# Scores and exponentials in padded rows of nine, divided into separate tiles

## The chip, the cores and the metric

The kernel runs on one core of one Trainium2 chip. The metric is the device time of one execution in microseconds; three runs of the kernel before gave a median of 691.24 us (690.34 to 692.95).

## The reference

Attention over 4 batches, 8 heads, 768 positions and 64 numbers per head, followed by an expert layer over 3072 tokens (512 to 2048 to 512):

```python
scores = scale * np.matmul(q, k.transpose(0, 1, 3, 2))
is_global = pos[None, :] < int(n_global)            # the first 8 keys
is_local = (rel >= 0) & (rel < int(n_local))        # 96 keys back
bias = -slopes[:, None, None] * dist[None, :, :]
scores = np.where(is_global | is_local, scores + bias[None], -1000000000.0)
a = np.exp(scores - np.max(scores, axis=-1, keepdims=True))
a = a / (np.sum(a, axis=-1, keepdims=True) + 1e-09)
x = np.matmul(a, v)            # then [tokens, 512]
h = x @ w_in
g = np.where(h > 0.0, h, np.exp(np.minimum(h, 0.0)) - 1.0)
out = g @ w_out
```

## The kernel before

The 3072 tokens are cut into 12 groups of 256 (two tiles of 128 queries), three groups to a batch. For each group four pairs of heads go through attention, and then 16 chunks of the expert layer (128 hidden columns each) follow. A tile of queries sees 232 keys (96 before it, the 8 global ones, its own 128); the first tile of a batch sees its own 128 alone.

Groups 0 to 3, counted from 0, run attention in plain float32 (`pair32`). From group 4 on, `pair` splits every operand of a matmul into a high part and a rest in a faster type, and works ahead: while TensorE goes through the expert chunks of one group, the attention of the next is threaded in between. There are 8 such groups and so 32 pairs of heads, each with four score tiles (two heads, two query tiles): 128 tiles, of which 16 have 128 columns and 112 have 232.

A pair goes like this. A *visit* of TensorE (L542 to L550) first transposes the probabilities of the pair before (L500, into the PSUM banks `t` and `th`) and then computes the scores of its own pair (L480, into `s`). VectorE adds the position table, takes the row maximum and writes maximum less score (L569) into a tile `pr`; ScalarE exponentiates it in place and sums the row (L571); VectorE inverts the sums (L584, L585) and multiplies each tile by its inverse, in place (L589 to L592, through L557): this is the division. The next visit transposes the tiles. Then ScalarE and VectorE split the transposed tiles (L517, L518), TensorE multiplies them with the values (L529, into `pv`), and VectorE adds the two halves (L536).

An expert chunk is eight or twelve matmuls into a PSUM bank `h` (L663, L667), a chain on ScalarE and VectorE (copy, L672, L683, L684, L685, a cast to `gh`), a subtraction to `gl` (L277, on GpSimd in this stretch), and matmuls that accumulate into two banks `o` (L707). There are two banks `h`, so the first matmul of a chunk waits until L685 has read the bank of the chunk but one before.

The order of all instructions on each engine is computed before the program is emitted. `Plan.order` (L102) takes, over and over, the operation that can start first, by written costs (`act`, `dve`, `pool`, `pe`), by due times, and by when a slot of the operation's tile class comes free. A cost is a triple of engine, time and a flag; an operation with the flag set waits, in this plan, until the last flagged operation has ended (`port`, L136 and L177). All GpSimd work carries the flag, and so does the division on VectorE. A visit is planned 1200 ns after its inputs are ready (`BEHIND`). `SLOTS` (L803) lists the buffers of each class: `pr` has four. On the chip the engines run their queues in the planned order and wait for each other by semaphores alone.

Of the kernel before, what the change touches and what calls it, by code (L numbers as in the profile page):

```python
# [11 lines left out]
AF = mybir.ActivationFunctionType  # L12
ALU = mybir.AluOpType
# [3 lines left out]
P = 128  # L17
# [3 lines left out]
WN = A0 + P  # L21
HK = WN // 2
NT = 2
# [183 lines left out]
def act(n, psum=False, extra=0.0):  # L207
    return (("ACT", (55 if psum else 97) + 0.834 * n + extra, False),)


def dve(n, fast=False, port=False):
    return (("DVE", (75 + 0.521 * n) if fast else (70 + 1.042 * n), fast or port),)


def pool(n, two=True):
    return (("POOL", (30 + 2.58 * n) if two else (50 + 1.1 * n), True),)
# [6 lines left out]
class Kernel:  # L223
# [182 lines left out]
    def pair(self, b, gi, hp, xh, xl, due, ahead, step, X):  # L406
        nc, p = self.nc, self.plan
        t0 = gi * NT
# [59 lines left out]
              [rqv, vd], [vd], due - 7500)  # L468

        ss = [self.bank("s", "s", [P, NT, WN]) for _ in range(2)]  # L470
        prs = [[self.sb("pr", "pr", [P, WN]) for _ in range(NT)] for _ in range(2)]
        st = self.sb("st", "st", [P, 3, 2 * NT])
        tiles = [(t0 + i, i * (NG + P)) + self.blocks(t0 + i) for i in range(NT)]
# [9 lines left out]
        self.visit(scores, 1.4 * sum(WN - x[2] for x in tiles), [qs, ks], ss, ahead)  # L483
        for j in range(2):
            for i in range(NT):
                self.softmax(b, 2 * hp + j, t0 + i, lambda j=j, i=i: ss[j].t[:, i], ss[j], prs[j][i], st, j * NT + i,
                             ahead + 7000 + (2 * j + i) * step)
        self.inverse(st, ahead + 4500 + 3 * step)
        for j in range(2):
            for i, x in enumerate(tiles):  # L490
                self.norm(prs[j][i], x[2], st, j * NT + i, ahead + 4600 + 3 * step + 2 * j + i, False)
        tps = [self.bank(c, c, [P, 2 * NT * 2, 64]) for c in ("t", "th")]

        def transposes():
# [66 lines left out]
    def softmax(self, b, h, t, st_, s, pr, st, i, d):  # L561

        nc, p = self.nc, self.plan
        lo = 0 if t else A0
        n = WN - lo
        at = (b * self.H + h) * (self.S // P) + t
        nm = self.nmax.t[:, at:at + 1]
        tab = self.tab1.t if t else self.tab0.t
        p.add((("DVE", 158 + 1.042 * n, False),), lambda e: nc.vector.tensor_tensor_reduce(  # L569
            pr.t[:, lo:], st_()[:, lo:], tab, -(2.0 ** -(h + 1)), 3.0e38, ALU.add, ALU.min, nm), [s], [pr], d - 4500)  # L570
        p.add(act(n, extra=200), lambda e: nc.scalar.activation(  # L571
            pr.t[:, lo:], pr.t[:, lo:], AF.Exp, bias=nm, scale=-1.0, accum_out=st.t[:, 0, i:i + 1]), [pr], [pr, st], d - 4000)

    def blocks(self, t):

# [10 lines left out]

        self.plan.add((("DVE", 290.0, False),), inverse, [st], [st], due)

    def norm(self, pr, lo, st, i, due, both):  # L589
        n = WN - lo  # L590
        self.plan.add((act(n, extra=90) + pool(n, False) if both else ()) + (("DVE", 130 + 0.53 * n, True),), lambda e: self.scaled(
            e, pr.t[:, lo:], pr.t[:, lo:], st.t[:, 2, i:i + 1]), [pr, st], [pr], due)  # L592

    def pair32(self, b, hp, t0, q32, k32, v32, rqv, rk, pv, due, step, X):

# [139 lines left out]
    def build(self):  # L735
# [49 lines left out]
        for _, f in sorted(todo, key=lambda x: x[0]):  # L785
# [16 lines left out]
    WARM, FILL = True, 60000.0  # L802
    SLOTS = {"rqv": ["rqv0"], "rk": ["rk0"], "qs": ["qs0"], "ks": ["ks0"], "vd": ["vd0", "part0", "part1"],  # L803
             "s": ["s0", "s1"], "t": ["t0"], "th": ["v0"], "pv": ["v0", "t0"], "h": ["h0", "h1"], "o0": ["o0"], "o1": ["o1"],
             "pr": ["pr0", "pr1", "pr2", "pr3"], "st": [f"st{i}" for i in range(6)], "pt": ["pt0", "pt1"],
             "x": ["x0"], "xh": ["xh0", "xh1", "xh2"], "e": ["e0", "e1"], "gh": ["gh0", "gh1", "gh2"],
             "gl": ["gl0", "gl1", "gl2"], "io": ["io0", "io1", "io2", "io3"], "part": ["part0", "part1", "vd0"]}

# [266 lines left out]
```

## Time and profile before

| What | Value |
|---|---|
| Median of three runs | 691.24 us |
| Profiled execution, its own time | 692.7 us |
| Its span, first to last instruction | 690.9 us |
| TensorE matmul busy | 677.5 us (98%) |
| VectorE busy | 510.0 us (74%) |
| ScalarE busy | 521.6 us (75%) |
| GpSimd busy | 219.7 us (32%) |
| Granted TensorE clock, mean | 0.999 |

The profile is of one execution. Busy times add the drawn lengths of the instructions, overlaps counted once. The drawn ends of matmuls are modelled, and consecutive ones overlap, so how far TensorE is from its best is read from when matmuls start, not from its busy share. "Idle before" names the time in which an engine had nothing drawn and what released it.

### The profile page before, as it was taken

What the parts mean: (1) busy time and instruction counts of PE and PEld (TensorE: products, weight loads), DVE (VectorE), ACT (ScalarE), POOL (GpSimd) and SP (SyncE); (2) the same over time, 40 slices, a digit from 0 to 9 for tenths busy, and PEclk for the clock granted to TensorE, in tenths of its full rate; (3) what the DMA queues carried; (4) which work ended last, traced back from release to release, by engine and by line L of the source; (5) the groups of instructions that cost most, each with busy time, mean ns of one, the idle gap of its engine ahead of it and who ended that gap; (6) DMA issues with size and microseconds to landing.
All of it is one profiled execution on the core that took longest, in us unless ns stands there. A gap on an engine that the chain in (4) does not pass through costs nothing.

```text
span 690.9 us, 13740 instructions
## 1 busy us (share of the span) xinstructions
PE 677.5 (98%) x4512; PEld 568.9 (82%) x4512; DVE 510.0 (74%) x1586; ACT 521.6 (75%) x1584; POOL 219.7 (32%) x304
## 2 busy tenths in 40 slices
PE   9999999999999999999999999999999999999996
PEld 6777888888888877788888888888888888888885
DVE  7999999985468777867876777777778766785322
ACT  7998888756477778778877888778778877886553
POOL 4142000200115433433353335333353443323221
PEclk9999999999999999999999999999999999999999
DMA  7837941001123112112212112112111211200001
GB/s 258 297 103 253 388 155 47 1 11 39 58 61 95 35 35 78 56 35 65 68 35 66 35 47 88 35 36 84 50 36 50 83 35 35 66 1 1 32 0 37
DMA packets 22402, 51.61 MB, mean 75 GB/s; under 512 B 2482, under 2 KB 9394, under 8 KB 22322
## 3 DMA queue, kind: packets, MB, share of 16 engines
q1 hardware_dynamic: 22176, 50.51, 22.0%
q8 instruction: 38, 0.62, 0.4%
q14 instruction: 42, 0.34, 0.2%
q10 hardware_dynamic: 146, 0.14, 0.1%
HBM read 44.34 MB, written 6.29 MB: 73 GB/s over the span
## 4 chain that ended last, share of the span: by engine, by line
PE 82%; DVE 8%; ACT 6%; issue 2%; DMA 1%; POOL 0%; DVEq 0%; POOLq 0%; ACTq 0%; SPq 0%
PE o L707 33%; PE h L663 16%; PE h L678 9%; PE h L667 8%; PE pv L529 3%; PE s L480 3%; PE t L500 2%; PE s L608 2%; ACT pr L571 2%; PE pv L642 1%; DVE x L536 1%; PE t L625 1%; DVE pr L557 1%; PE none L851 1%; DMA rqv<-in_qkv_dram 1%
## 5 line engine op out<-in xcount | busy, mean ns | idle before, releaser
L707 PE MATMUL o<-w,gh 128*128 128x512 f32 x764 | 227.6, 398 | 0.6 <-DVE part L723 0.4
L277 POOL TENSOR_TENSOR gl<-e,gh 128x256 fp32r<-128x256 f32 x144 | 108.4, 753 | 214.3 <-ACT gh L269 199.4
L707 PEld LDWEIGHTS o<-w,gh 128*128 128x128 f32 x764 | 135.4, 188 | 26.7 <-ACT gh L269 0.8
L663 PE MATMUL h<-xh,w 128*128 128x512 f32 x568 | 155.4, 395 | 2.1 <-DVE e L685 1.9
L685 DVE SCALAR_TENSOR_TENSOR e<-e,h 128x256 f32<-128x256 f32 x192 | 80.3, 418 | 70.6 <-ACT e L684 64.5
L663 PEld LDWEIGHTS h<-xh,w 128*128 128x128 f32 x568 | 104.7, 188 | 29.5 <-DVE e L685 5.3
L707 PE MATMUL o<-w,gl 128*128 128x512 f32 x382 | 129.0, 398 | 0.0
L269 ACT CAST gh<-e 128x256 fp32r<-128x256 f32 x192 | 77.9, 406 | 53.6 <-DVE e L685 52.7
L683 ACT ACTIVATE e<-h 128x256 f32<-128x256 f32 x192 | 74.0, 386 | 52.9 <-DVE h L672 34.7
L571 ACT ACTIVATE pr<-pr,nmax 128x232 f32<-128x232 f32 (+1 forms) x192 | 91.4, 478 | 6.0 <-DVE nmax L569 5.9
L667 PEld LDWEIGHTS h<-xh,w 128*128 128x128 f32 x568 | 86.1, 188 | 11.7
L672 DVE TENSOR_TENSOR h<-h,e 128x256 f32<-128x256 f32 x142 | 60.9, 429 | 45.4 <-ACT e L269 44.8
L678 PEld LDWEIGHTS h<-xh,w 128*128 128x128 f32 x600 | 85.6, 189 | 9.6 <-issue 1.9
L678 PE MATMUL h<-xh,w 128*128 128x256 f32 x600 | 92.4, 284 | 0.0
L667 PE MATMUL h<-xh,w 128*128 128x256 f32 x568 | 89.6, 280 | 0.0
L684 ACT ACTIVATE e<-e 128x256 f32<-128x256 f32 x192 | 80.4, 419 | 4.1
L569 DVE CUSTOM_DVE_ANT_0 pr<-s,tab 128x232 f32<-128x232 f32 (+1 forms) x192 | 67.1, 375 | 15.4 <-PE s L480 15.0
L269 ACT COPY e<-h 128x256 f32<-128x256 f32 x142 | 53.1, 374 | 20.2 <-PE h L667 15.9
L707 PEld LDWEIGHTS o<-w,gl 128*128 128x128 f32 x382 | 63.9, 189 | 4.8 <-issue 0.3
L536 DVE TENSOR_TENSOR x<-pv,x 64x256 f32<-64x256 f32 x128 | 53.8, 420 | 9.1 <-ACT x L269 6.5
L557 DVE TENSOR_SCALAR pr<-pr,st 128x232 f32<-128x232 f32 (+1 forms) x143 | 58.2, 433 | 0.9
L559 POOL TENSOR_SCALAR pr<-pr,st 128x232 f32<-128x232 f32 (+1 forms) x31 | 17.2, 566 | 104.5 <-DVE st L585 54.8
(108 smaller groups left out, 903.0 us busy)
## 6 DMA issues: line engine op xcount, KB each, us to landing
rqv<-in_qkv_dram SPq DMA_DIRECT2D x45, 384.0 KB, 3.1
rk<-in_qkv_dram SPq DMA_DIRECT2D x45, 184.0 KB, 2.6
bits<-in_w_in_dram SPq DMA_DIRECT2D x16, 512.0 KB, 7.2
bits<-in_w_out_dram SPq DMA_DIRECT2D x16, 512.0 KB, 9.9
out_dram<-ob SPq DMA_DIRECT2D x24, 256.0 KB, 2.0
rqv<-in_qkv_dram SPq DMA_DIRECT2D x3, 192.0 KB, 5.1
rqv<-in_qkv_dram SPq DMA_DIRECT2D x3, 128.0 KB, 2.7
rk<-in_qkv_dram SPq DMA_DIRECT2D x2, 132.0 KB, 3.5
```

The costliest lines, as they stand in the source:

```text
L269: self.nc.scalar.copy(out, x)
L277: self.on(e).tensor_tensor(out, x, y, ALU.subtract)
L557: self.nc.vector.tensor_scalar(out, x, sc, None, ALU.mult)
L569: p.add((("DVE", 158 + 1.042 * n, False),), lambda e: nc.vector.tensor_tensor_reduce(pr.t[:, lo:], st_()[:, lo:], tab, -(2.0 ** -(h + 1)), ...
L571: p.add(act(n, extra=200), lambda e: nc.scalar.activation(pr.t[:, lo:], pr.t[:, lo:], AF.Exp, bias=nm, scale=-1.0, accum_out=st.t[:, 0, i: ...
L663: nc.tensor.matmul(h.t, w1.t[:, HI, cc * P:(cc + 1) * P], xh.t[:, :, cc], start=cc == 0, stop=False)
L667: nc.tensor.matmul(hx(), w1.t[:, LO, cc * P:(cc + 1) * P], xh.t[:, HI, cc], start=False, stop=cc == self.NCC - 1)
L678: nc.tensor.matmul(hx(), w1.t[:, s, cc * P:(cc + 1) * P], xh.t[:, x, cc], start=n == 0 and cc == 0, stop=n == 2 and cc == self.NCC - 1)
L683: p.add(act(W, True), lambda e: nc.scalar.activation(ex.t, hx(), AF.Relu, scale=-1.0), [h], [ex], d - 8000)
L684: p.add(act(W), lambda e: nc.scalar.activation(ex.t, ex.t, AF.Exp, scale=-1.0), [ex], [ex], d - 8000)
L685: p.add(dve(W), lambda e: nc.vector.scalar_tensor_tensor(ex.t, ex.t, -1.0, hx(), ALU.add, ALU.max), [h, ex], [ex], d - 8000)
L707: nc.tensor.matmul(acc[i].t, g.t[:, i * P:(i + 1) * P], w2.t[:, s], start=fc == f0 and n == 0 and s == HI, stop=fc == f1 - 1 and n == 1)
```

## The change

From group 4 on, L569 and L571 work in tiles `raw` of their own, of 29 rows of 9 numbers of which 8 are used (16 rows for a tile of 128 columns). The division reads a `raw` tile and writes a `pr` tile as one contiguous run. In the plan the wide divisions (29 rows, an odd number) get the cost `dve(n)` without the flag; those of 128 columns keep the old cost. The classes `pr` and `raw` share six slots. Groups 0 to 3 keep their tiles; the helper `eights` leaves their operands one run. The new lines are L570 (scores), L573 (exponentials) and L558 (division).

```diff
+        raws = [[self.sb("raw", "raw", [P, WN // 8, 9]) for _ in range(NT)] for _ in range(2)]
         prs = [[self.sb("pr", "pr", [P, WN]) for _ in range(NT)] for _ in range(2)]
...
-                self.softmax(b, 2 * hp + j, t0 + i, lambda j=j, i=i: ss[j].t[:, i], ss[j], prs[j][i], st, j * NT + i,
+                self.softmax(b, 2 * hp + j, t0 + i, lambda j=j, i=i: ss[j].t[:, i], ss[j], raws[j][i], st, j * NT + i,
...
-                self.norm(prs[j][i], x[2], st, j * NT + i, ahead + 4600 + 3 * step + 2 * j + i, False)
+                self.norm(prs[j][i], x[2], st, j * NT + i, ahead + 4600 + 3 * step + 2 * j + i, False, raws[j][i])
...
-            pr.t[:, lo:], st_()[:, lo:], tab, -(2.0 ** -(h + 1)), 3.0e38, ALU.add, ALU.min, nm), [s], [pr], d - 4500)
+            self.eights(pr.t, n, lo), self.eights(st_()[:, lo:], n), self.eights(tab, n), -(2.0 ** -(h + 1)), 3.0e38, ALU.add, ALU.min, nm),
+            [s], [pr], d - 4500)
...
-            pr.t[:, lo:], pr.t[:, lo:], AF.Exp, bias=nm, scale=-1.0, accum_out=st.t[:, 0, i:i + 1]), [pr], [pr, st], d - 4000)
+            self.eights(pr.t, n, lo), self.eights(pr.t, n, lo), AF.Exp, bias=nm, scale=-1.0, accum_out=st.t[:, 0, i:i + 1]),
+            [pr], [pr, st], d - 4000)
...
-    def norm(self, pr, lo, st, i, due, both):
+    def eights(self, x, n, lo=0):
+
+        if len(x.shape) == 3:
+            return x[:, :n // 8, :8]
+        return x[:, lo:lo + n].rearrange("p (a b) -> p a b", b=8)
+
+    def norm(self, pr, lo, st, i, due, both, raw=None):
+
         n = WN - lo
-        self.plan.add((act(n, extra=90) + pool(n, False) if both else ()) + (("DVE", 130 + 0.53 * n, True),), lambda e: self.scaled(
-            e, pr.t[:, lo:], pr.t[:, lo:], st.t[:, 2, i:i + 1]), [pr, st], [pr], due)
+        x = raw or pr
+        one_port = raw and n // 8 % 2
+        self.plan.add((act(n, extra=90) + pool(n, False) if both else ()) + (dve(n) if one_port else (("DVE", 130 + 0.53 * n, True),)),
+                      lambda e: self.scaled(e, self.eights(pr.t, n, lo), self.eights(x.t, n, lo), st.t[:, 2, i:i + 1]), [x, st], [pr], due)
...
-             "pr": ["pr0", "pr1", "pr2", "pr3"], "st": [f"st{i}" for i in range(6)], "pt": ["pt0", "pt1"],
+             "pr": ["pr2", "pr3", "pr0", "pr1", "raw0", "raw1"], "raw": ["raw0", "raw1", "pr0", "pr1"], "st": [f"st{i}" for i in range(6)], "pt": ["pt0", "pt1"],
```

On VectorE, the order changes around the divisions. These rows are from the second pair of heads of group 4, from the sums (`st`) on; `x` is the output of L536, `h` and `e` belong to expert chunks, `ks` is the next pair's keys. Before:

```order
L585 RECIPROCAL st_2852<-st_2852 128x4
L536 TENSOR_TENSOR x_2911<-pv_2903,x_2911 64x256
L672 TENSOR_TENSOR h_2913<-h_2913,e_2945 128x256
L536 TENSOR_TENSOR x_2911<-pv_2903,x_2911 64x256
L277 TENSOR_TENSOR ks_2880<-rk_2750,ks_2880 128x368
L557 TENSOR_SCALAR pr_2838<-pr_2838,st_2852 128x232
L685 SCALAR_TENSOR_TENSOR e_2945<-e_2945,h_2913 128x256
L557 TENSOR_SCALAR pr_2846<-pr_2846,st_2852 128x232
L557 TENSOR_SCALAR pr_2874<-pr_2874,st_2852 128x232
L557 TENSOR_SCALAR pr_2918<-pr_2918,st_2852 128x232
```

After:

```order
L588 RECIPROCAL st_2856<-st_2856 128x4
L558 TENSOR_SCALAR pr_2946<-raw_2842,st_2856 128x232
L558 TENSOR_SCALAR pr_2953<-raw_2850,st_2856 128x232
L537 TENSOR_TENSOR x_2915<-pv_2907,x_2915 64x256
L684 TENSOR_TENSOR h_2917<-h_2917,e_2951 128x256
L537 TENSOR_TENSOR x_2915<-pv_2907,x_2915 64x256
L277 TENSOR_TENSOR ks_2884<-rk_2750,ks_2884 128x368
L558 TENSOR_SCALAR pr_2974<-raw_2878,st_2856 128x232
L558 TENSOR_SCALAR pr_2982<-raw_2922,st_2856 128x232
L697 SCALAR_TENSOR_TENSOR e_2951<-e_2951,h_2917 128x256
```

Two divisions stand ahead of the additions and the key subtraction, and all four ahead of the chunk's L697 (L685 before).

On TensorE, the visits move. These rows are the end of the expert matmuls that lie between the second and the third visit of that group, up to the first transposes of the third. Before:

```order
L707 MATMUL o_2942<-w_126_1034,gl_3129 128x512
L707 MATMUL o_2927<-w_285_1253,gh_3145 128x512 x2
L707 MATMUL o_2942<-w_285_1253,gh_3145 128x512 x2
L667 MATMUL h_3149<-xh_2320,w_294_1316 128x256 x4
L707 MATMUL o_2927<-w_285_1253,gl_3156 128x512
L707 MATMUL o_2942<-w_285_1253,gl_3156 128x512
L707 MATMUL o_2927<-w_291_1365,gh_3167 128x512 x2
L663 MATMUL h_3187<-xh_2320,w_300_1392 128x512 x4
L707 MATMUL o_2942<-w_291_1365,gh_3167 128x512 x2
L667 MATMUL h_3187<-xh_2320,w_300_1392 128x256 x4
L500 MATMUL t_3204<-ident,pr_3043 116x64
L500 MATMUL th_3205<-ident,pr_3043 116x64
```

After:

```order
L719 MATMUL o_2948<-w_126_1034,gh_3122 128x512 x2
L679 MATMUL h_3131<-xh_2320,w_288_1236 128x256 x4
L719 MATMUL o_2931<-w_126_1034,gl_3137 128x512
L719 MATMUL o_2948<-w_126_1034,gl_3137 128x512
L675 MATMUL h_3166<-xh_2320,w_294_1316 128x512 x4
L501 MATMUL t_3178<-ident,pr_3127 116x64
L501 MATMUL th_3179<-ident,pr_3127 116x64
```

The third visit comes right after the first half of the chunk that uses `w_294`; before, that chunk's second half, the next chunk's matmuls and twelve of L707 stood ahead of it. The number of expert matmuls in the group stays as it was; the gap before the next group's first visit gets those that the earlier gaps lose.

## Rows read from the trace of the kernel before

**Rows 1.** the page, shares of the chain that ended last, by engine:

```profile
PE 82%; DVE 8%; ACT 6%; issue 2%; DMA 1%; POOL 0%; DVEq 0%; POOLq 0%; ACTq 0%; SPq 0%
```

**Rows 2.** waits in 195:640: engine, line, releaser: total us, times, longest:

```profile
PEld h L663 <- DVE e L685: 5.3, 14, 1.1
PE h L663 <- DVE e L685: 1.9, 5, 0.7
PE th L500 <- DVE x L536: 0.9, 1, 0.9
```

**Rows 3.** TensorE: start, us, what, count; then a group, its mean ns:

```profile
418.10 1.08 PE L707 MATMUL o<-w,gh 128*128 128x512 f32 x4
419.02 0.63 PE L667 MATMUL h<-xh,w 128*128 128x256 f32 x4
...
L707 PE MATMUL o<-w,gh 128*128 128x512 f32 x522 | 154.7, 399 | 0.0
```

**Rows 4.** TensorE in order of time; in brackets idle before, releaser:

```profile
213.45 0.73 PE L663 MATMUL h<-xh,w 128*128 128x512 f32 x2 [0.29 <-DVE e L685]
...
255.64 0.24 PE L500 MATMUL th<-ident,pr 64*116 64x64 f32 x1 [0.86 <-DVE x L536]
...
281.72 0.96 PE L663 MATMUL h<-xh,w 128*128 128x512 f32 x3 [0.70 <-DVE e L685]
...
498.55 0.47 PE L663 MATMUL h<-xh,w 128*128 128x512 f32 x1 [0.35 <-DVE e L685]
...
610.67 0.27 PE L500 MATMUL t<-ident,pr 64*116 64x64 f32 x1
```

**Rows 5.** VectorE and GpSimd in order of time, before three of these waits:

```profile
212.04 0.90 DVE L557 TENSOR_SCALAR pr<-pr,st 128x232 f32<-128x232 f32 x1
...
212.07 0.74 POOL L277 TENSOR_TENSOR xh<-x,xh 128x256 fp32r<-128x256 f32 x1 [1.44 <-ACT xh L269]
...
252.69 1.88 DVE L557 TENSOR_SCALAR pr<-pr,st 128x232 f32<-128x232 f32 x2
...
253.13 1.30 POOL L277 TENSOR_TENSOR vd<-rqv,vd 128x512 fp32r<-128x512 f32 x1
...
278.95 1.35 DVE L557 TENSOR_SCALAR pr<-pr,st 128x232 f32<-128x232 f32 x2
...
279.00 1.16 POOL L277 TENSOR_TENSOR vd<-rqv,vd 128x384 fp32r<-128x384 f32 x1
```

**Rows 6.** L557: ns least/median/longest; then its wide form in 195:640, mean ns:

```profile
L557 DVE TENSOR_SCALAR pr<-pr,st x143: 269/336/1462, 9.0 to 619.4; 128x232 f32<-128x232 f32 x127, 128x128 f32<-128x128 f32 x16
...
L557 DVE TENSOR_SCALAR pr<-pr,st 128x232 f32<-128x232 f32 x112 | 47.8, 449 | 0.6
```

**Rows 7.** VectorE groups by line and shape: busy us, mean ns, idle before:

```profile
L459 DVE SCALAR_TENSOR_TENSOR qs<-rqv,scale,qs 128x256 fp32r<-128x256 f32 x31 | 14.9, 482 | 0.2
...
L387 DVE SCALAR_TENSOR_TENSOR g<-bits,g 128x512 int32<-128x512 int32 x32 | 21.8, 684 | 0.0
...
L277 DVE TENSOR_TENSOR w<-g,w 128x512 fp32r<-128x512 f32 x26 | 17.8, 684 | 0.0
...
L277 DVE TENSOR_TENSOR ks<-rk,ks 128x368 fp32r<-128x368 f32 x24 | 12.9, 537 | 0.1
```

**Rows 8.** ScalarE groups by line and shape:

```profile
L571 ACT ACTIVATE pr<-pr,nmax 128x232 f32<-128x232 f32 x160 | 78.6, 492 | 1.3 <-DVE nmax L569 1.2
...
L378 ACT ACTIVATE g<-bits 128x512 f32<-128x512 f32 x32 | 21.4, 675 | 1.3 <-DVE w L277 0.6 <-DMA bits<-in_w_in_dram 0.6
L269 ACT CAST w<-g 128x512 fp32r<-128x512 f32 x32 | 19.8, 619 | 3.4 <-DVE g L387 3.3
```

**Rows 9.** three gaps between visits: length, busy us (instructions) of each engine:

```profile
243.73:254.51 10.78, 10.78 (x79) 9.13 (x79) 9.29 (x27) 8.23 (x27) 3.88 (x5) 1.00 0.18 56
599.60:610.67 11.07, 11.07 (x80) 9.30 (x80) 9.25 (x30) 8.72 (x29) 2.32 (x3) 1.00 0.00 0
610.67:621.04 10.37, 10.37 (x77) 8.88 (x76) 8.19 (x29) 8.91 (x28) 2.94 (x4) 1.00 0.01 2
```

## The prediction

> **What bounds the kernel now.** I read the chain of waits first, then who waited for whom in the stretch that the change touches, then single instructions in order of time where TensorE waited. The chain that ended last lies on TensorE for 82%, on VectorE for 8% and on ScalarE for 6% of the span [rows 1]. So nothing but a wait of TensorE is worth anything. The division that the change rewrites (L557 in the groups from 4 on, counted from 0) runs between 195 and 640 us; there TensorE shows idle time before two lines only: 1.9 us in five waits before L663 (the first matmul of an expert chunk, which needs the PSUM bank that VectorE's L685 reads) and 0.9 us in one wait before the transposes L500 [rows 2]. Matmuls overlap: one with 512 columns is drawn about 0.40 us long, but four in a row start 0.23 us apart (418.10 to 419.02 is 0.92 for four) [rows 3]. A wait therefore hides 0.40 - 0.23 = 0.17 us more than its idle time shows. Six waits: 1.9 + 0.9 + 6 x 0.17 = 3.8 us. That is about all the change can win. The outer bound is what the weight loads show: 5.3 us before L663 in 14 waits, plus the 0.9 = 6.2 us [rows 2].
>
> Why do these waits exist? At 255.64 us the transposes into bank th had waited 0.86 us for an addition L536, which stood in VectorE's queue behind two divisions that together took 1.88 us; all that time GpSimd had a subtraction of 1.30 us running (253.13 to 254.43), and the divisions end 0.14 us after it. At 281.72 the wait of 0.70 us has two divisions of 1.35 us before it, beside a GpSimd subtraction of 1.16 us (to 280.16); at 213.45, 0.29 us, one of 0.90 us beside GpSimd's 0.74 us [rows 4, 5]. The division has a median of 336 ns and a longest of 1462 ns [rows 6]: it is an instruction that sometimes stands still until GpSimd is done. The three waits are 0.86 + 0.70 + 0.29 + 3 x 0.17 = 2.4 us; the other three (1.9 + 0.9 - 1.85 = 0.95 shown, 1.5 with the hidden part) have no long division right before them.
>
> **The division.** 112 of the 128 divisions have 232 columns, 16 have 128. Today the 112 have a mean of 449 ns [rows 6], so 112 x (449 - 336) = 12.7 us of VectorE's time go into standing still. After the change the source is 29 rows of 8 with a gap, the destination one run of 232. No row shows what that does, so I bound it. From below: nothing changes, 336 ns and the standing still as now. [...] Two subtractions of the same kind differ by (684 - 537) / (512 - 368) = 1.02 ns per element; an instruction with a per-row scalar from a tile and 256 elements at that rate takes 482 ns [rows 7], so 232 elements take 482 - 24 x 1.02 = 457 ns. I take 457 ns, nearest to the L459 row, without standing still: 112 x (457 - 449) = 0.9 us more VectorE time over 445 us, so nothing in sum, but every division costs the same and none costs 1.46 us. The 16 narrow divisions have 16 rows, and I leave them at what they cost now.
>
> [...]
>
> **The padded tiles.** L569 writes and L571 reads and writes 29 rows of 8 instead of a run. Nearest rows: L387 reads every second word and takes 684 ns for 512 elements, the contiguous subtraction also 684 [rows 7], so VectorE pays 0. ScalarE's L378 reads every second word in 675 ns, its contiguous cast L269 takes 619 [rows 8]; if all of the 56 ns were the stride, 232 elements would pay 25 ns, at both ends of the instruction 50. I take 0; the other end is 4 x 50 = 0.2 us per pair of heads on the way from scores to transposes. A gain here has no reason.
>
> **The buffers and the order.** Six slots stand where four did, a score tile is free again after its division, and the planner no longer holds a wide division back for GpSimd. The divisions move forward on VectorE, ahead of the additions L536 (the first order piece), and the next visit of the transposes comes sooner on TensorE (the second). Between visits TensorE has expert matmuls; counted in the two orders, the four gaps of the first group hold 40, 42, 42, 30 matmuls of 512 columns before and 38, 30, 30, 56 after; in the later ones without a first tile the pattern is 34, 36, 30, 60. Matmuls neither come nor go, so TensorE's work stays. SP's loads keep their sequence. On GpSimd the value tiles of the next pair come ahead of one or two expert subtractions; those are then late by that much, and hidden by the chunk of matmuls that TensorE still has between a chunk's first and last use. New waits: L569 waits for a division two or more instructions back on its own engine, which has ended by then; behind it would stand the following scores and L672, but I price it at 0.
>
> A gap with 30 to 31 matmuls exists today: 243.73 to 254.51 and 599.60 to 610.67, followed by one of 10.37 us. VectorE is busy 9.29 of 10.78, 9.25 of 11.07 and 8.19 of 10.37 us in them [rows 9]. The first ends in the 0.86 us wait; the transposes at 610.67 show no idle before them [rows 4]. So a short gap is kept without a wait when the divisions do not stand still. Cover for a late division is the time that VectorE has free: 2.18 us in the third of these gaps; four divisions that are each 457 - 336 = 0.12 us slower than a quiet one use 0.5 of it, the padded tiles at worst 0.2.
>
> **Sum.** Of the three waits with a long division before them 2.4 us go; of the other 1.5 us about half, 0.7, since divisions earlier in the queue delay them as well; against this the shorter gaps, where I count 11 with 30 or 34 matmuls and put 0.04 us on each, a third of the 0.12 us by which one division is slower than a quiet one: 0.4 us. 2.4 + 0.7 - 0.4 = 2.7 us. The profiled execution took 692.7 us (span 690.9 and 1.8 around it), so 690.0 for such a run. The median of the runs shown, 691.24, lies 1.46 below the profiled run; the forecast on that footing is 688.5 us, with its own range 687.0 to 690.3.
>
> **Rivals.**
> 1. All waits go, and some hidden ones with them: between 3.8 and 6.2 us, say 4.6, gives 686.6. For it: the long divisions are the only irregular instruction of VectorE there. Against: L663 also waits after chains without a long division (498.55).
> 2. Another wait takes over at once: L685 still comes behind ScalarE, and TensorE loses what it won. 691.2 us. For it: three of the six waits have no long division right before them.
> [...]
> 4. Slower: the shorter gaps. Three visits follow each other closely; the loop from scores over L569, L571, L584, L557 to the next transposes must run in about 11 us. It decides from the point where the loop is longer than the gap: then each of the six gaps with 30 matmuls ends in a wait like that at 255.64, 1.03 us, and the five with 34 in half of one: 6 x 1.03 + 5 x 0.5 = 8.7, less the 3.8 won: 4.9 us more, 696.1. For it: of today's three gaps with at most 32 matmuls, two end in a wait. Against: both have a division beside GpSimd, the third has not and does not wait.
>
> **Chances.** Forecast 0.44, rival 1 0.25, rival 2 0.14, rival 3 0.05, rival 4 0.12. Half a per cent (3.46 us, about what a measurement of this kernel tells from no change) means under 687.8 or over 694.7. Faster: rival 1 and a small part of the forecast, 0.30. Slower: most of rival 4 and a rest, 0.11. Same: 0.59. The range 686.2 to 693.0 leaves out rival 4 and the far end of rival 1.
>
> **What will show it.** Right: L558, the new division, wide form, within 440 to 475 ns, its longest under 600; no idle before the transposes; 1 us or less before the expert matmuls that now wait 1.9. VectorE's busy time changed by under 5 us. L573, the exponential in its new form, within 50 ns of 492 [rows 8]. Wrong: a wide division still over 800 ns (rival 3), exponentials over 550 ns, or repeated idle before the transposes at the end of gaps of about 11 us (rival 4).

## The result and the profile after

The change made the kernel slower: 698.85 us (median of six runs, 697.35 to 699.68) against 691.98 us for the kernel before on the same chip (six runs, 690.34 to 693.58), a ratio of 1.0097 with the interval 1.0078 to 1.0115. The prediction said 688.5. The profiled execution took 699.68 us, with a span of 697.7.

The shares of the chain that ended last [rows 1] are now:

```profile
PE 78%; DVE 11%; ACT 7%; issue 2%; DMA 1%; POOL 0%; DVEq 0%; POOLq 0%; ACTq 0%; SPq 0%
```

TensorE has lost four points of it and VectorE has won three. Where it happens, TensorE's waits from 195 to 650 us show (what waited, for whom, total us, times, longest; PEld is TensorE's weight load), to be read against [rows 2]:

```profile
PE h L675 <- DVE e L697: 6.8, 13, 1.0
...
PEld h L675 <- DVE e L697: 9.0, 13, 1.5
```

One line is left: the first matmul of an expert chunk (L675, L663 before) waits for VectorE's L697 (L685 before), 6.8 us against 1.9. The wait before the transposes is gone. From start to start, less the usual distance of such matmuls (medians: 0.23 us after one of 512 columns, 0.12 after one of 256), 14 of these waits are over 0.15 us and add up to 9.1 us; before there were eight of 3.4 us in all, and the one before the transposes with 1.1. The difference is 4.6 us.

The operations that were rewritten, on VectorE and ScalarE from 195 to 640 us by shape (busy us, mean ns, then the idle time before them), to be read against [rows 6] and [rows 8]:

```profile
L558 DVE TENSOR_SCALAR pr<-raw,st 128x232 f32<-128x232 f32 x112 | 47.3, 443 | 0.6
L570 DVE CUSTOM_DVE_ANT_0 raw<-s,tab 128x232 f32<-128x232 f32 x112 | 41.6, 393 | 14.0 <-PE s L481 14.0
```

```profile
L573 ACT ACTIVATE raw<-raw,nmax 128x232 f32<-128x232 f32 x112 | 55.1, 493 | 0.0
```

The division has the mean that it had (443 ns, 449 before) by another road: no wide one takes over 456 ns, where the quiet median was 336 and the longest 1462. Of all 128 divisions (ns least, median, longest, and when), the longest is a narrow one:

```profile
L558 DVE TENSOR_SCALAR pr<-raw,st x128: 269/442/824, 199.3 to 621.9; 128x232 f32<-128x232 f32 x112, 128x128 f32<-128x128 f32 x16
```

The scores took 393 ns in the old tiles as well, the exponentials 495 in this stretch.

Two of the short gaps between visits, which the new order made (length, then busy us of PE, PEld, DVE, ACT and POOL, each with its instructions, clock, DMA), to be read against [rows 9]:

```profile
217.46:229.29 11.83, 11.09 (x80) 9.03 (x79) 9.55 (x30) 9.55 (x30) 5.96 (x8) 1.00 0.17 49
229.29:240.88 11.59, 11.07 (x79) 9.06 (x79) 9.54 (x30) 9.34 (x30) 4.76 (x7) 1.00 0.16 52
```

Each holds one of the waits, four matmuls ahead of the gap's end. The chain of waits before the first of them (start, us, what):

```profile
224.68 0.46 DVE pr L558
225.13 0.32 DVE x L537
225.45 0.34 DVE h L684
225.79 0.32 DVE x L537
226.11 0.98 DVE pr L558 x3
227.10 0.14 issue
227.23 0.43 DVE x L537
227.66 0.03 issue
227.69 0.43 DVE e L697
228.12 0.04 issue
228.17 0.96 PE h L675 x3
```

By its drawn lengths VectorE has no gap over 0.05 us here: L697 comes after four divisions, three additions L537 and L684, the chunk's own earlier step. ScalarE had finished the exponential that L697 needs at 227.04 (226.62 + 0.42), so L697 started 0.65 us later than it could:

```profile
226.62 0.42 ACT L696 ACTIVATE e<-e 128x256 f32<-128x256 f32 x1
...
226.04 1.16 DVE L558 TENSOR_SCALAR pr<-raw,st 128x232 f32<-128x232 f32 x3
```

On TensorE, four matmuls L675 and then the transposes are queued behind it:

```profile
226.81 0.62 PE L719 MATMUL o<-w,gl 128*128 128x512 f32 x2
228.17 1.19 PE L675 MATMUL h<-xh,w 128*128 128x512 f32 x4 [0.74 <-DVE e L697]
229.29 0.27 PE L501 MATMUL t<-ident,pr 64*116 64x64 f32 x1
```

The last of the divisions (226.04 + 1.16 = 227.20) is done 2.1 us before the transposes that read it. Work that had time stands ahead of work that had none.

### The profile page after: what moved, and what is told of

Same layout as the page of the kernel before. It is cut to its first block, busy times and chain, and to the rows that moved or that the text cites. A ratio compares the mean times of both kernels' runs of the same rounds, so it can differ in the third digit from the quotient of the medians.

```text
span 697.7 us, 13749 instructions
## 1 busy us (share of the span) xinstructions
PE 680.3 (97%) x4512; PEld 569.3 (82%) x4512; DVE 504.9 (72%) x1586; ACT 526.8 (76%) x1584; POOL 218.2 (31%) x304
## 4 chain that ended last, share of the span: by engine, by line
PE 78%; DVE 11%; ACT 7%; issue 2%; DMA 1%; POOL 0%; DVEq 0%; POOLq 0%; ACTq 0%; SPq 0%
PE o L719 31%; PE h L675 16%; PE h L690 9%; PE h L679 8%; PE s L481 3%; PE pv L530 3%; PE t L501 2%; DVE pr L558 2%; PE s L620 2%; DVE e L697 2%; DVE x L537 2%; ACT raw L573 2%; PE t L637 1%; PE pv L654 1%; PE none L863 1%
## 5 line engine op out<-in xcount | busy, mean ns | idle before, releaser
L719 PE MATMUL o<-w,gh 128*128 128x512 f32 x764 | 228.4, 399 | 0.5 <-DVE part L735 0.4
L277 POOL TENSOR_TENSOR gl<-e,gh 128x256 fp32r<-128x256 f32 x144 | 106.8, 741 | 211.1 <-ACT gh L269 186.0
L675 PE MATMUL h<-xh,w 128*128 128x512 f32 x568 | 155.8, 396 | 6.9 <-DVE e L697 6.8
L719 PEld LDWEIGHTS o<-w,gh 128*128 128x128 f32 x764 | 134.8, 188 | 26.4 <-ACT gh L269 0.7
L697 DVE SCALAR_TENSOR_TENSOR e<-e,h 128x256 f32<-128x256 f32 x192 | 80.2, 418 | 81.8 <-ACT e L696 71.7
L675 PEld LDWEIGHTS h<-xh,w 128*128 128x128 f32 x568 | 104.9, 188 | 36.6 <-DVE e L697 9.0
L719 PE MATMUL o<-w,gl 128*128 128x512 f32 x382 | 127.3, 396 | 0.0
L684 DVE TENSOR_TENSOR h<-h,e 128x256 f32<-128x256 f32 x142 | 60.8, 428 | 48.3 <-ACT e L269 47.1
L719 PEld LDWEIGHTS o<-w,gl 128*128 128x128 f32 x382 | 63.6, 188 | 4.2 <-issue 0.3
L573 ACT ACTIVATE raw<-raw,nmax 128x232 f32<-128x232 f32 (+1 forms) x128 | 61.6, 484 | 0.0
L570 DVE CUSTOM_DVE_ANT_0 raw<-s,tab 128x232 f32<-128x232 f32 (+1 forms) x128 | 45.7, 380 | 18.4 <-PE s L481 18.4
L537 DVE TENSOR_TENSOR x<-pv,x 64x256 f32<-64x256 f32 x128 | 53.5, 418 | 3.4 <-ACT x L269 1.2
L558 DVE TENSOR_SCALAR pr<-raw,st 128x232 f32<-128x232 f32 (+1 forms) x128 | 52.6, 436 | 0.9
L271 POOL CAST vd<-rqv 128x512 fp32r<-128x512 f32 (+1 forms) x32 | 18.8, 586 | 103.6 <-PE pv L530 71.5
```

The lines of the kernel that those rows point to most:

```text
L277: self.on(e).tensor_tensor(out, x, y, ALU.subtract)
L537: p.add(dve(W), lambda e, pv=pv, r=r, y=y: nc.vector.tensor_tensor(xt(r), pv.t[r, :, y], xt(r), ALU.add), [pv, x], [x], due + 600 + 2 * y + j)
L558: self.nc.vector.tensor_scalar(out, x, sc, None, ALU.mult)
L573: p.add(act(n, extra=200), lambda e: nc.scalar.activation(self.eights(pr.t, n, lo), self.eights(pr.t, n, lo), AF.Exp, bias=nm, scale=-1.0, ...
L675: nc.tensor.matmul(h.t, w1.t[:, HI, cc * P:(cc + 1) * P], xh.t[:, :, cc], start=cc == 0, stop=False)
L697: p.add(dve(W), lambda e: nc.vector.scalar_tensor_tensor(ex.t, ex.t, -1.0, hx(), ALU.add, ALU.max), [h, ex], [ex], d - 8000)
```

## The experiments

The theories of the first seven runs are four: the *forms* (new operands, new tiles, their slots) cost time; the *price* that the planner gives a wide division (`dve(232)` = 312 ns, where three in a row start 0.36 us apart) makes an order that VectorE can't keep; the visits that now follow each other closely cost time by themselves; or any new order would be about as bad. As a second measure beside the median I use one stretch of the profiles, from the first transposes L501 to the hundredth matmul into `h` from the end: the work in it is the same in every kernel but e6 and e7, and ahead of it TensorE's order is the same before and after. In e6 and e7 two of its matmuls L719 stand ahead of it; their 0.46 us are added back in the table. It takes 449.8 us before (200.94 to 650.71) and 454.6 after (203.03 to 657.60), 4.8 more, of which the waits above are 4.6. Each stretch is of one execution, the ratio is of several; where the two measures differ, I give both.

| Run | Ratio to before (95%) | Stretch, us, less before |
|---|---|---|
| after, first measurement | 1.0097 (1.0078 to 1.0115) | +4.8 |
| after again (e8) | 1.0086 (1.0070 to 1.0103) | +4.8 |
| e1 new forms, old order | 0.9995 (0.9983 to 1.0008) | -1.2 |
| e2 new order, old form of the division | 1.0241 (1.0208 to 1.0275) | +15.1 |
| e3 price 372 | 0.9986 (0.9972 to 1.0000) | -1.4 |
| e4 price 312 with the flag | 1.0132 (1.0112 to 1.0153) | +8.8 |
| e5 new order, 184 columns divided | 1.0071 (1.0054 to 1.0088) | +1.2 |
| e6 price 402 | 0.9980 (0.9971 to 0.9990) | -2.3 |
| e7 price 492 | 0.9979 (0.9968 to 0.9990) | -2.2 |
| e9 L697 moved forward | 1.0035 (1.0018 to 1.0051) | +1.5 |
| e10 TensorE swapped in five gaps | 1.0059 (1.0038 to 1.0079) | +3.0 |
| e11 both edits | 1.0035 (1.0020 to 1.0050) | +1.9 |
| e12 one division behind L697 | 1.0044 (1.0032 to 1.0057) | +2.0 |
| e13 e12 and e10 together | 1.0019 (1.0006 to 1.0031) | +0.4 |

**e1, the new forms in the old order.** The planner is told the old price and flag; every engine's order is that of before.

```diff
-(dve(n) if one_port else (("DVE", 130 + 0.53 * n, True),))
+(("DVE", 130 + 0.53 * n, True),)
```

> [...] Theory A (the order costs, the instructions do not): not slower than before, ratio 0.993 to 1.000; the 2.4 us of waits behind long divisions go. Theory B (the slower division, 0.36 instead of 0.25 us of VectorE's time, makes the chunk's L697 late): most of the 1.0% loss stays, ratio 1.005 to 1.010, and TensorE's idle before the expert chunks is near 7 us.

Measured: 691.85 us against 692.62. The waits of TensorE from 195 to 650 us:

```profile
PE h L675 <- DVE e L697: 1.0, 4, 0.4
PE o L719 <- POOL gl L277: 0.2, 1, 0.2
```

This is theory A. The forms cost nothing and take 1.2 us out of the stretch, half of the 2.4 that were expected to go. The loss is in the order.

**e2, the new order with the old form of the division.** Rows of 8 instead of 9, so the division is one run on both sides again.

```diff
-[P, WN // 8, 9]
+[P, WN // 8, 8]
```

> [...] Theory A: slower than before by as much as the changed kernel or more (ratio 1.007 to 1.015), since the divisions also stand still beside GpSimd. Theory B: near before, 0.998 to 1.004, since the division is fast again.

Measured: 709.28 us, beyond what either theory allowed. The wide divisions now have a mean of 525 ns (195 to 650 us; below it, all divisions with ns least, median, longest, and when):

```profile
L558 DVE TENSOR_SCALAR pr<-raw,st 128x232 f32<-128x232 f32 x112 | 56.5, 525 | 0.6
...
L558 DVE TENSOR_SCALAR pr<-raw,st x128: 269/335/1462, 198.4 to 631.0; 128x232 f32<-128x232 f32 x112, 128x128 f32<-128x128 f32 x16
```

and the wait of TensorE:

```profile
PE h L675 <- DVE e L697: 16.1, 15, 1.8
```

The new order with a division that stands still costs three times as much as with one that doesn't (15.1 us of the stretch against 4.8), at the same place: a late VectorE is dear in it.

**e3, a price just above the true distance** (372 ns, where divisions in a row start 0.36 us apart).

```diff
-dve(n) if one_port
+(("DVE", 130 + 1.042 * n, False),) if one_port
```

> The changed kernel, with 130 + 1.042 n (372 ns) for the wide division in the plan, in place of 70 + 1.042 n (312 ns); measured are 362 ns of VectorE's time. If the waits come from the plan's too low price (Theory A1), they shrink to under 3 us idle and the ratio to before falls under 1.003. If they come from the close visits as such (Theory A2), the order hardly differs (one gap of 30 matmuls becomes 34) and the ratio stays at 1.006 to 1.011.

Measured: 691.88 us.

```profile
PE h L675 <- DVE e L697: 1.5, 4, 0.7
```

Sixty ns more in one price, and the loss is gone. It also speaks on the visits: counted in the traces as matmuls of 512 columns between one visit and the next, the change has seven gaps of 30 and seven of 34, and e3 has six of 30 and eight of 34. Its visits are as close, and it loses nothing: that they follow each other closely is not what costs.

**e4, the low price with the flag.** Here the planner again holds a wide division back until GpSimd is done, so the visits lie further apart, with 32 to 50 matmuls of 512 columns between them.

```diff
-dve(n) if one_port
+dve(n, port=True) if one_port
```

> The changed kernel with its price for the division (312 ns), but with the flag that makes the plan wait for GpSimd. The visits then lie further apart (gaps of 44, 44, 42, 40, 50, 40, 38, 34 matmuls in the first two groups, no 30). Theory A2 (close visits cost): ratio 0.993 to 1.002. Theory B: 1.005 to 1.010 as in the changed kernel.

Measured: 701.97 us, slower than the change itself, with other waits:

```profile
PE o L719 <- ACT gh L269: 3.2, 4, 1.5
PE h L675 <- DVE e L697: 3.2, 5, 1.0
PE h L675 <- POOL xh L277: 2.2, 3, 1.1
```

It is outside the range of either theory. Wide gaps at the low price lose more, by waits that the change does not have (for ScalarE's `gh`, for GpSimd's `xh`), so this order differs in more than the gaps and is no clean test of close visits; e3 is. What makes it worse I did not follow further.

**e5, a cheaper division in the new order.** Each wide division handles 184 of its 232 columns (48 are left out) and takes 393 ns instead of 443; three in a row start 0.31 us apart instead of 0.36, which is the price of 312. Four memsets at the start fill the unwritten parts.

```diff
-self.scaled(e, self.eights(pr.t, n, lo), self.eights(x.t, n, lo), ...
+self.scaled(e, self.eights(pr.t, 184 if one_port else n, lo), self.eights(x.t, 184 if one_port else n, lo), ...
```

> [...] If the loss comes from the 50 ns by which each division outlasts its price (Theory A1), TensorE's idle before the expert chunks falls from 6.8 us to about 2 and the stretch from the first to the last visit from 423.0 to about 418. If it comes from the order itself whatever the division costs (Theory A2), the stretch stays above 421 us.

Measured: 696.68 us, and the same waits, most of them shorter by 0.15 to 0.25 us (6.6 instead of 9.1 us from start to start):

```profile
PE h L677 <- DVE e L699: 4.1, 11, 0.8
```

Idle time before the expert chunks is 4.1 us, where about 2 or still 6.8 were expected, and the stretch from the first to the last visit 419.9, between the 418 and 421: neither theory alone. Fifty ns per division are worth 2.6 us by the waits, 3.6 by the stretch of one execution, but 1.8 of 6.5 by the medians (against e8). So between a quarter and three quarters of the loss is the difference between what the planner thought a division takes and what it took; the rest goes with the order.

**e6 and e7, prices of 402 and 492 ns, and e8, the change measured again.**

```diff
-dve(n) if one_port
+(("DVE", 160 + 1.042 * n, False),) if one_port
```

with 250 for e7.

> The changed kernel with 160 + 1.042 n (402 ns) as the plan's price of the wide division, above what it takes. Theory A1: waits stay away, ratio to before 0.996 to 1.001, as with 372 ns. A third theory, that the planner is so sensitive that any new number moves the time by a per cent either way (Theory C), allows anything from 0.99 to 1.015.

> The same with 250 + 1.042 n (492 ns), a third above what it takes. Theory A1: no worse than 1.002, since too high a price only spreads the visits. Theory C: anything from 0.99 to 1.015.

> The changed kernel once more, for a second profile: of the 6.8 us by which its span was longer, 1.9 lay before 23 us, where both kernels run the same program. If that is the load of that one execution, it is gone here and the ratio falls to 1.007 to 1.010; if it belongs to the kernel, the first visit is again at 203 us.

Measured: 690.51, 690.96 and 698.46 us, against 692.0. The waits of e6, then of the change again:

```profile
PE h L675 <- DVE e L697: 1.2, 6, 0.2
```

```profile
PE h L675 <- DVE e L697: 6.9, 13, 1.0
```

Three prices from 372 up give three orders of which none is slower than before: a new order as such is no loss. e6 and e7 are the versions that beat both kernels, by 0.2%; e3 can't be told from no change. A price under the true distance is not enough for a loss either: e1's plan has 253 ns (130 + 0.53 x 232) with the flag, some 110 under the distance, and loses nothing. What the price decides is which order comes out. e8 falls in the range expected for it; its first visit is at 201.96 us, between the two answers.

The next runs keep the change's own plan and undo it at the places that the trace names, on one engine each.

**e9 and e11, L697 ahead of the last division.**

```diff
+if j < k - 1 and kind(on[j]) == "D" and kind(on[j - 1]) == "D":
+    order.remove(op)                       # op: L697
+    order.insert(order.index(on[j]), op)   # on[j]: the last division ahead of it
```

> The changed kernel's plan; then, on VectorE alone, L697 is taken out at the 16 places where two or three wide divisions and one or two of the additions L537 stand right ahead of it, and put ahead of the last of these divisions. Nothing else moves, TensorE's order included. Theory A (L697 is late because it is queued behind divisions and additions; in the changed kernel's trace it starts 0.42 to 0.80 us after its exponential L696 has ended at these places): 13 of the 14 waits over 0.15 us before L675, 7.9 of their 9.1 us, lie behind such a place, and each loses 0.3 to 0.5 us, so about 5 us: 693 to 695 against 698.5, and no wait before the transposes, which had 1.6 us to spare. Theory B (what decides is TensorE's order, in which the next chunk's first matmuls stand ahead of two that are ready): the waits that TensorE's order makes stay, under 2 us gained. Theory C (L697 waits for ScalarE's exponential anyway): nothing, 698 to 699.

> Both edits on the changed kernel's plan. Theory A: L697 is 0.3 to 0.5 us earlier and TensorE has 0.46 us of other work in five of the gaps, so of the 9.1 us of waits some 3 stay: 692 to 693.5, about the kernel before. If there is a further cost in the changed kernel's order that does not show in these waits, the time stays over 695.

Measured: 694.62 and 694.51 us. These two do not settle the question. At nine of the 16 places the edit put L697 ahead of its own exponential in the program, so it read the numbers before the exponential and did not wait for ScalarE (in the trace nine of L697 start before their exponential has ended); their times are those of a shorter chain. e12 and e13 do it with every dependency kept.

**e10, two ready matmuls first.** On TensorE, at five gaps that end in four L675, two L719 (which read `gl`) and a visit, the two go first, as the order of e3 has it.

```diff
+if kind(op) == "u" and next_two == "gg" and then_a_visit:   # u: L675, g: L719 with gl
+    order.remove(op)
+    order.insert(order.index(on[k + 2]) + 1, op)
```

> The changed kernel's plan; then, on TensorE alone, at the gaps that end in four L675, two L719 that read gl, and a visit, the two L719 go ahead of the four L675, as the plan with the true price of the division has them. Nothing else moves. Theory B (TensorE's order decides): these are the gaps behind the waits of about 0.7 us (270.30, 379.20, 544.26, 600.32); two matmuls of 0.23 us stand in each, so 0.46 us each, five gaps, 2.3 us: 696 against 698.5. Theory A (the queue of VectorE alone): the same 0.46 us of cover, so about 2.3 us too, but the other nine waits stay as they are. If TensorE is held by something else there: nothing.

Measured: 696.11 us, 2.3 us under e8, as expected (4.5 over its own before, where e8 was 6.5 over). One of the five places, after:

```profile
269.09 0.62 PE L719 MATMUL o<-w,gh 128*128 128x512 f32 x2
270.30 1.16 PE L675 MATMUL h<-xh,w 128*128 128x512 f32 x4 [0.58 <-DVE e L697]
271.30 0.63 PE L719 MATMUL o<-w,gl 128*128 128x512 f32 x2
```

and in e10:

```profile
267.59 0.63 PE L719 MATMUL o<-w,gh 128*128 128x512 f32 x2
268.06 0.63 PE L719 MATMUL o<-w,gl 128*128 128x512 f32 x2
268.80 1.17 PE L675 MATMUL h<-xh,w 128*128 128x512 f32 x4
```

Two L719 take 0.46 us. After, L675 starts 1.21 us after the pair ahead of it (270.30 - 269.09), 0.75 too late; in e10 0.74 us (268.80 - 268.06), 0.28 too late. VectorE was no earlier: L697 starts 0.64 us after the start of that pair in both. TensorE spent the 0.46 us of two ready matmuls ahead of the wait instead of behind it. About a third of the loss is this.

**e12 and e13, one division behind L697.** At the same 16 places the last division goes right behind L697; e13 adds the edit of e10.

```diff
+    order.remove(on[j])                        # the last division
+    order.insert(order.index(op) + 1, on[j])   # right behind L697
```

> The changed kernel's plan; then, on VectorE alone, at the 16 places where two or three wide divisions and one or two additions L537 stand right ahead of L697, the last of these divisions goes right behind L697 (the additions stay). TensorE's order is the changed kernel's. Theory A (L697 is late by the divisions ahead of it): L697 starts up to 0.39 us earlier (the distance of two divisions) at each place, as its exponential has ended 0.42 to 0.80 us before it; 13 of the 14 waits before L675 lie behind such a place, so 13 times 0.35 to 0.39, some 4.5 to 5 us: 693.5 to 694.5 against 698.5. If TensorE's order alone decides: under 1 us gained, 698.

> The last division behind L697 at 16 places, and at five gaps the two L719 that read gl ahead of the four L675. If the waits before L675 carry the whole loss: 2 us less than with the first edit alone where the waits of those gaps are still over 0.3 us, so 691.5 to 693, the kernel before. If the changed order costs something else besides, over 695.

Measured: 695.19 and 693.82 us, against 692.05. VectorE in e12 before the wait that stood at 228.17 after:

```profile
224.11 0.80 DVE L558 TENSOR_SCALAR pr<-raw,st 128x232 f32<-128x232 f32 x2
224.94 0.43 DVE L537 TENSOR_TENSOR x<-pv,x 64x256 f32<-64x256 f32 x1
225.41 0.42 DVE L697 SCALAR_TENSOR_TENSOR e<-e,h 128x256 f32<-128x256 f32 x1
225.74 0.45 DVE L558 TENSOR_SCALAR pr<-raw,st 128x232 f32<-128x232 f32 x1
```

and TensorE there:

```profile
224.88 0.62 PE L719 MATMUL o<-w,gl 128*128 128x512 f32 x2
225.88 1.19 PE L675 MATMUL h<-xh,w 128*128 128x512 f32 x4 [0.38 <-DVE e L697]
227.01 0.27 PE L501 MATMUL t<-ident,pr 64*116 64x64 f32 x1
```

The wait is 0.38 us where it was 0.74, by one division's 0.36, and the transposes still wait for nothing. In the stretch e12 gives back 2.8 of 4.8 us and e13 4.4. In medians e12 is 3.1 us and e13 1.8 us over before, where e8 was 6.5 over: half, and nearly three quarters. Both miss the range expected for them (693.5 to 694.5, 691.5 to 693) by under 1 us. The waits that stay in e13 are fewer but not gone:

```profile
PE h L675 <- DVE e L697: 3.1, 5, 1.0
```

Three of them, 2.6 us, stand ahead of the first group's visits (at 214.47, 226.40 and 238.32 us). At 214.47 two divisions stand right ahead of L697 with no addition between them, a place that the edit passes over. At 226.40, where e12 has the 0.38 us above, the wait is 0.81, because L587, the small addition to the sums, took 0.61 us, beside a cast on GpSimd that ended 0.03 us before it:

```profile
222.41 0.61 DVE L587 TENSOR_SCALAR st<-st 128x4 f32<-128x4 f32 x1
...
222.38 0.61 POOL L271 CAST vd<-rqv 128x512 fp32r<-128x512 f32 x1 [4.07 <-PE pv L530]
```

In e12 the same L587 took 0.17 us, 0.44 less. The change ended such long instructions among the wide divisions (longest 456 ns, 1462 before) and left them at L587: its median is 170 ns and its longest 1069 (170 and 1075 before).

## Why the prediction was wrong, step by step

- **The division.** Right. 443 ns for a forecast of 457, the longest 456, none standing still, where a quiet one took 336 before and the longest 1462. The 457, and the 2.4 us of waits that were to go, assume that the new operands run at the rate of the L459 row and never stand still: that was an estimate of mine, no run before the change shows it, and none shows why they do. What the runs show in its place: of the wide divisions 28 of 112 took over 456 ns before and none after; the narrow form, of 16 rows, still has four over 500 ns, up to 824 (three before, up to 818); and the waits brought 1.2 us in the stretch (e1). Rival 3, in which wide divisions go on taking over 800 ns, is out; e2, which has such divisions in the new order, shows that its price was far too low besides: 709.28 instead of 692.7.
- **The padded tiles.** Right, at 0: 393 and 493 ns.
- **The waits removed.** In kind right, in size too large. In the old order (e1) they bring 1.2 us in the stretch, not 2.4 + 0.7, and 0.8 us in the medians, which can't be told from none.
- **The buffers and the order.** This is the step that failed. The sum has one term for the new order, the shorter gaps, 0.4 us in all, and looks for it at the transposes at the end of a gap. The change's first piece of the order showed that all four divisions now stand ahead of L697, and I priced what moved forward and not what it pushed back. L697 feeds the bank that TensorE's next chunk waits for; it has no spare time, where a division had 2.1 us. I also took the price of a division for a detail of the planner. I had forecast 457 ns and saw `dve(n)` = 312 in the diff, and did not ask what a plan is worth that is 50 ns short at every division (0.36 us apart against 312 ns): with up to four of them ahead of L697 that makes it late by up to 0.2 us (an estimate from these two numbers) of the 0.65 us at 228.17. In its place the runs show 4.8 us more in the stretch; taking one division from in front of L697 gives back 2.8 (e12), two matmuls moved on TensorE 1.8 (e10), both 4.4 (e13), and a price that fits gives back all and 1.4 to 2.3 more (e3, e6, e7). The kernel before had already shown this kind of wait. I read the one at 281.72 us as a wait for divisions that stand still; the rows after the divisions of 278.95 [rows 5] show two more additions ahead of L685, which started 1.34 us after its exponential had ended (279.48 + 0.42):

```profile
279.48 0.42 ACT L684 ACTIVATE e<-e 128x256 f32<-128x256 f32 x1
...
280.32 0.89 DVE L536 TENSOR_TENSOR x<-pv,x 64x256 f32<-64x256 f32 x2
281.24 0.42 DVE L685 SCALAR_TENSOR_TENSOR e<-e,h 128x256 f32<-128x256 f32 x1
```

- **Rival 4.** Its sign was right and its size near (696.1, a chance of 0.12), its place was wrong, so the nearness is luck. It put the wait before the transposes; none is there. Its count was short too: the trace has seven gaps of 30 matmuls and seven of 34, not six and five (before, four and not three gaps have at most 32). The short gaps were kept, with VectorE busy 9.55 of 11.83 us. The wait came up inside the same gaps, at the expert chunk.
- **The signs to look for.** 6.8 us before the expert matmuls where 1 or less was forecast: that alone says the step is wrong. VectorE's busy time fell by 5.1 us, just past the 5 I allowed, and ScalarE's rose by 5.2. With the drawn lengths simply added, VectorE's fall by 2.7 us and ScalarE's by 1.1: ScalarE does no more work, its instructions overlap less.
- **What stays open.** Some 2 us of the 6.9 lie outside the stretch in the profiled execution (the first transposes at 203.03 us, 200.94 before), where the order on TensorE is the same; in e8 it was 201.96, and over the executions of the others it goes from 200.65 (e1) to 202.51 (e5), and to 203.06 in e6, a faster kernel, which has two matmuls more ahead of it. I can't tell a cost from chance there.

## What to carry to other kernels

When an edit moves instructions forward in an engine's queue, price what they push back: find the first instruction behind them whose reader is the bottleneck, and how late it gets; and check whether the thing moved had time to spare. A planner's price is part of the kernel: if an operation's form changes, measure its new distance first and set the price at it or a little above. Here 312 ns lost 0.9 to 1.0% and 372, 402 and 492 lost nothing; one such planner does not show how far that carries. An operation that is the same in sum but without stalls (431 to 456 ns, instead of a median of 336 with up to 1462) gained nothing that can be told from noise in the old order (e1), and 0.2% in an order made for its new length (e6, e7).

## What was not expected of the hardware

Rows of 8 numbers at a distance of 9 cost neither VectorE nor ScalarE anything, as forecast: 393 ns for the scores in both kinds of tiles, 493 and 495 for the exponentials. Not forecast was e2. Without the gap, where divisions stand still again (up to 1462 ns), the new order gives wide divisions of 525 ns on the mean, where the old order had 449. The quiet ones took the same (medians of all divisions 335 and 336 ns), so the time that divisions stood still went with the order here, and a plan made for the new form did not fit the old one: 709.28 us.
